# Two last attention groups, two chunks of batch 1's split input and 70 due times put elsewhere in a planned one-core kernel

## The chip, the core and the metric

The program runs on one core of a Trainium2 chip. The time is the device time of the whole program in microseconds (us), the median over several executions. The engines of the core are TensorE (PE in the profile, with its weight loads as PEld), VectorE (DVE), ScalarE (ACT), GpSimd (POOL) and SyncE (SP), which here only issues transfers. Each engine runs its own list of instructions in order and waits on semaphores for the others.

## The reference, cut to what is computed

```python
# 1 attention with feature maps: 8 batches, 8 heads, 576 rows, head_dim 64, 128 features
proj = q_or_k @ w_phi;  proj -= max(abs(proj), -1);  phi = concat(exp(proj), exp(-proj))
kv = einsum('bhsf,bhsd->bhfd', phi_k, v);  z = sum(phi_k, axis=2)
x = (phi_q @ kv) / (phi_q @ z + 1e-6)            # heads joined: x is [8, 576, 512]
# 2 gated mixer
gate = sigmoid(sum over k < 5 of conv_w[k] * shifted(x, k))
x = (gate * (x @ w_val)) @ w_out
# 3 Fourier mixing and MLP
u  = x + real(fft(fft(x, axis=1), axis=2))
un = (u - mean(u)) / sqrt(var(u) + 1e-6)
return u + maximum(un @ w_ch1, 0) @ w_ch2
```

Everything is float32. Products that need the precision are made of a high and a low part of the inputs, three matmuls for each product.

## The kernel before

The kernel has two halves. The first, up to 286 us of the trace, is attention: batches and heads in groups, in an order written out by hand. Of its steps only the end matters here. `emit_yT` (line 306) transposes the features of q on TensorE (tile `yt`), `emit_qE` lets ScalarE take the exponentials (`qe`), `emit_KV` (line 284) accumulates `kv` and copies it to `kvT`, `emit_num` makes the numerator (`nm`), VectorE divides (`xs`), `emit_XT` transposes back (`xt`, line 349), `emit_xT` copies that out of its bank (`xT`), and SP stores it to the scratch `x_scr`, from where the mixer loads its input `xf`.

The second half is one list of 4629 operations. The functions `note_...` write them down in program order with what each reads and writes, and `place_ops` (line 1165) turns them into the lists of the engines: backwards it gives each operation a due time, then it goes forward and takes, on each engine, the operation that is ready with the earliest due time. An operation can be allowed on two engines (letters `v`, `p`, `a`, `m`, `d` for VectorE, GpSimd, ScalarE, TensorE, SP); the forward pass then chooses. `key_at` and `free` say how far resources and engines are already taken when the list begins.

For each batch b of eight the list holds:

- `note_x` (line 519): the input is split in four chunks c into a high part (ScalarE) and a low part (VectorE or GpSimd, `o_lo`), into the tile pair `xh`. One pair serves all batches, so a chunk is written only after the batch before has read it for the last time.
- `note_taps`, `note_V` (line 545): the gate, and for each of four column groups m the product `val` = x @ w_val, in two halves of the sequence, one in each of the banks `val0` and `val1`. VectorE multiplies by the gate into `gv` and back into the bank, copies a column, and adds and subtracts the halves into `gs`. When that is done the bank is free for the next product. The split of `gs` is `ge`.
- `note_W`: the product of `ge` with w_out, into the banks `ps`. `note_FD` is the transform over features (tiles `f`, `Y`, rests `md`, `xr`, `rem`), `note_SD` the one over the sequence.
- `ln_first`: the LayerNorm of the first rows, whose mean is a product of `sh` and `sl` (a row block's high and low part) with ones. `note_sums` works off sums of weights (`ws`, four additions on GpSimd, a store `s_scr<-ws` and a load `ws<-s_scr`), beside everything else.

The tail of attention (`note_tail`: the last groups' `yt`, `kv`, `nm`, `xt`) is part of this list; the generator `tail` is stepped once for each m of batch 0. Which tiles exist when is set by `STAGES` (line 657): an operation with a key of stage 2 runs only after `open_mix2` (line 449) has made that stage's tiles, and `open_mix2` begins with six memsets on GpSimd. The list then goes on to the MLP, which fills the second half of the span.

## Time and profile before

| | us |
|---|---|
| median of 3 runs | 1323.23 (1321.36 to 1324.6) |
| profiled execution, its own time | 1319.18 |
| span of that execution in the trace | 1317.1 |
| PE busy | 1285.5 |
| DVE busy | 1134.1 |
| ACT busy | 919.0 |
| POOL busy | 791.9 |

The profile is of one execution; what lies outside its span is 2.1 us. PE busy counts matmuls from their start to a modelled end. A gap on an engine is printed in brackets, with the releaser: the engine and the tile whose instruction ended the wait. The granted clock (PEclk) is 1.00 at 2.4 GHz and 0.50 at 1.2 GHz.

### The profile page before, as it was taken

What the parts mean: (1) busy time and instruction counts of PE and PEld (TensorE: products, weight loads), DVE (VectorE), ACT (ScalarE), POOL (GpSimd) and SP (SyncE); (2) the same over time, 40 slices, a digit from 0 to 9 for tenths busy, and PEclk for the clock granted to TensorE, in tenths of its full rate; (3) what the DMA queues carried; (4) which work ended last, traced back from release to release, by engine and by line L of the source; (5) the groups of instructions that cost most, each with busy time, mean ns of one, the idle gap of its engine ahead of it and who ended that gap; (6) DMA issues with size and microseconds to landing.
All of it is one profiled execution on the core that took longest, in us unless ns stands there. A gap on an engine that the chain in (4) does not pass through costs nothing.

```text
span 1317.1 us, 30740 instructions
## 1 busy us (share of the span) xinstructions
PE 1285.5 (98%) x11952; PEld 1183.3 (90%) x11952; DVE 1134.1 (86%) x1771; ACT 919.0 (70%) x1718; POOL 791.9 (60%) x661
## 2 busy tenths in 40 slices
PE   8999999998999998999999999999999999999998
PEld 7999899988999998998888888888888888889997
DVE  6888888878889889779989989998989888888785
ACT  6888999774556546466867687767677676777662
POOL 4868889333557666464665755597458856583321
PEclk9999999998999999999999999999999999999999
DMA  8689999522342442528433653356333743345322
GB/s 309 207 287 308 319 300 296 189 83 89 137 165 88 147 155 89 177 89 276 138 102 102 222 159 104 103 160 218 104 103 117 241 123 100 105 149 182 105 84 89
DMA packets 147005, 214.62 MB, mean 163 GB/s; under 512 B 18854, under 2 KB 105382, under 8 KB 146860
## 3 DMA queue, kind: packets, MB, share of 16 engines
q1 hardware_dynamic: 142400, 203.06, 47.5%
q10 hardware_dynamic: 4460, 9.62, 2.0%
q8 instruction: 93, 1.52, 0.5%
q14 instruction: 52, 0.43, 0.1%
HBM read 165.63 MB, written 46.99 MB: 161 GB/s over the span
## 4 chain that ended last, share of the span: by engine, by line
PE 86%; DVE 6%; ACT 4%; DMA 2%; issue 1%; POOL 0%; SPq 0%; DVEq 0%; POOLq 0%; ACTq 0%
PE x L64 15%; PE cx L64 15%; PE ps L64 12%; PE cy L64 11%; PE y L64 8%; PE val L64 5%; PE kv L64 5%; PE pj L64 5%; PE nm L64 4%; PE z L64 4%; DVE acc L64 2%; PE yt L311 2%; PE xt L349 1%; ACT qe L64 1%; DMA r<-s_scr 1%
## 5 line engine op out<-in xcount | busy, mean ns | idle before, releaser
L64 POOL TENSOR_TENSOR r<-r 128x256 fp32r<-128x256 f32 (+1 forms) x301 | 293.4, 992 | 245.6 <-ACT r L64 229.2
L64 ACT ACTIVATE r<-r 128x256 fp32r<-128x256 f32 (+1 forms) x420 | 195.3, 487 | 53.4 <-DMA r<-s_scr 49.7
L64 PE MATMUL x<-un,r 128*128 128x462 f32 (+1 forms) x960 | 221.2, 371 | 2.2 <-ACT c L64 1.4
L64 PE MATMUL cx<-h,r 128*128 128x462 f32 (+1 forms) x960 | 213.9, 371 | 1.1 <-DVE acc L64 1.1
L64 PEld LDWEIGHTS x<-un,r 128*128 128x128 f32 x960 | 180.4, 188 | 23.5 <-ACT c L64 1.8
L64 PEld LDWEIGHTS cx<-h,r 128*128 128x128 f32 x960 | 180.2, 188 | 22.1 <-DVE acc L64 1.8
L64 PE MATMUL cy<-h,r 128*128 128x462 f32 (+1 forms) x720 | 159.9, 370 | 0.0
L64 PEld LDWEIGHTS cy<-h,r 128*128 128x128 f32 x720 | 135.3, 188 | 15.1
L64 PE MATMUL val<-xh,wv 128*128 128x290 f32 x768 | 118.0, 303 | 10.6 <-DVE gs L64 4.7
L64 PEld LDWEIGHTS val<-xh,wv 128*128 128x128 f32 x768 | 108.5, 193 | 13.7 <-DVE gs L64 5.6
L64 PE MATMUL y<-un,r 128*128 128x462 f32 (+1 forms) x480 | 113.9, 372 | 0.4 <-DVE h L64 0.4
L64 PE MATMUL ps<-ge,wo 128*128 128x290 f32 x768 | 107.3, 297 | 2.0 <-DVE x L64 1.1
L64 PEld LDWEIGHTS ps<-ge,wo 128*128 128x128 f32 x768 | 104.5, 189 | 2.8 <-DVE x L64 1.3
L270 DVE TENSOR_REDUCE m<-pj 128x6 f32<-128x768 f32 x96 | 91.5, 953 | 15.4 <-PE pj L64 14.8
L64 PEld LDWEIGHTS y<-un,r 128*128 128x128 f32 x480 | 90.0, 188 | 11.4 <-DVE h L64 1.1
L64 DVE SCALAR_TENSOR_TENSOR acc<-xf,cw,acc 128x576 f32<-128x576 f32 x112 | 91.4, 816 | 10.0 <-ACT acc L64 9.1
L64 DVE TENSOR_TENSOR acc<-cx,acc 128x924 f32<-128x924 f32 (+1 forms) x80 | 88.9, 1112 | 11.6 <-PE cx L64 10.2
L271 DVE TENSOR_TENSOR y<-pj,m 128x768 f32<-128x768 f32 x96 | 91.9, 958 | 6.9 <-DVE m L270 0.5
L64 PE MATMUL kv<-vraw,ke 128*64 128x66 f32 x2560 | 88.1, 224 | 1.7 <-ACT kvT L64 1.7
L64 ACT ACTIVATE qe<-yt 128x768 f32<-128x768 f32 x96 | 72.6, 812 | 23.4 <-PE yt L311 23.4
L64 ACT ACTIVATE h<-z 128x462 fp32r<-128x462 f32 (+1 forms) x120 | 66.4, 553 | 29.8 <-DVE z L64 26.1
L64 PE MATMUL pj<-wp,kqraw 64*128 64x128 f32 x1152 | 80.8, 287 | 6.0 <-DMA kqraw<-in_k_dram 4.0
(174 smaller groups left out, 2752.5 us busy)
## 6 DMA issues: line engine op xcount, KB each, us to landing
r<-s_scr SPq DMA_DIRECT2D x280, 128.0 KB, 2.4
r<-s_scr SPq DMA_DIRECT2D x140, 256.0 KB, 2.6
raw<-in_w_ch_dram SPq DMA_DIRECT2D x32, 512.0 KB, 6.0
vraw<-in_v_dram SPq DMA_DIRECT2D x32, 330.0 KB, 6.1
u_scr<-u ACTq DMA_DIRECT2D x8, 1152.0 KB, 6.3
kqraw<-in_k_dram SPq DMA_DIRECT2D x46, 192.0 KB, 4.1
kqraw<-in_q_dram SPq DMA_DIRECT2D x46, 192.0 KB, 3.7
s_scr<-mt SPq DMA_DIRECT2D x32, 256.0 KB, 5.2
```

What stands on the lines that cost most here:

```text
L64: return lambda *a, **k: f(*(resolve(x) for x in a), **{n: resolve(x) for n, x in k.items()})
L270: nc.vector.tensor_reduce(out=m, in_=pv, axis=AX.X, op=ALU.max, apply_absolute_value=True)
L271: nc.vector.tensor_tensor(out=y, in0=pv, in1=m.unsqueeze(3).to_broadcast([128, 2, CH, F]), op=ALU.subtract)
L311: nc.tensor.transpose(t[:, h, j * F:(j + 1) * F], y[:, h, j, :], ident)
L349: nc.tensor.transpose(t[:, 0, j * F:(j + 1) * F], x[:, j].rearrange("p h d -> p (h d)"), ident)
```

## The change

Six things are changed. The copy of the last `kv` is an operation of its own. The tail is stepped twice at m = 0 and m = 1 and not at m = 2 and 3. Chunks 0 and 1 of batch 1's split input go to other places: three slices of 576 columns of the tile of `Y` (now one tile for both halves of the feature transform) and one in the tile of `sh0` and `sl0` (now one tile, `sums0`). They get the key `xq` of stage 2, and batch 1's first product counts as a reader of `Y`, `sh0` and `sl0`, so nothing writes these before it is done. The eviction `xT` may go to VectorE or ScalarE. The planner starts with ScalarE taken for 1.4 us, VectorE for 0.7 and the bank `tr` until 1.4, and makes three backward passes instead of two. And a table MOVES shifts the due times of 70 operations (numbers 7 to 1498 of 4629) by multiples of 0.5 us, the largest by 191 us.

```diff
@@ -281,7 +281,12 @@
 
     KV_PARTS = [[[(0, 0), (1, 1), (2, 2)]], [[(3, 0), (4, 1)], [(5, 1), (6, 2)]], [[(7, 0), (8, 1), (9, 2)]]]
 
-    def emit_KV(i, part):
+    def copy_KV(u, b):
+        if b == 0:
+            kvT[u] = sm_p.tile([128, 4, 2, 65], F32, tag="kvT", name="kvT")
+        act.activation(out=kvT[u][:, :, b, :], in_=kvps.pop((u, b))[:, :, 0:65], func=ACTF.Copy)
+
+    def emit_KV(i, part, copy=True):
         u, g = divmod(i, NG)
         tv = vraw[u % 2]
         e = kE[i]
@@ -296,10 +301,8 @@
                     for p in HALVES:
                         mm(t[p, w, :], e[:, a, h, j, p], tv[:, h, slot, :],
                            start=slot % 5 == 0 and w == 0, stop=slot % 5 == 4 and w == 3, skip_group_check=True)
-            if slot % 5 == 4:
-                if b == 0:
-                    kvT[u] = sm_p.tile([128, 4, 2, 65], F32, tag="kvT", name="kvT")
-                act.activation(out=kvT[u][:, :, b, :], in_=kvps.pop((u, b))[:, :, 0:65], func=ACTF.Copy)
+            if slot % 5 == 4 and copy:
+                copy_KV(u, b)
         if part == len(KV_PARTS[g]) - 1:
             kE.pop(i)
 
@@ -452,12 +455,17 @@
         late["fs"] = x2.tile([128, 2, NE], F32, name="fs")
         late["c256"] = x2.tile([128, 5, 128], F32R, name="c256")
         late["r256"] = x2.tile([97, 2, NE], F32, name="r256")
+        sums = x2.tile([128, 2, HB], F32R, name="sums0")
+        Y = x2.tile([128, 2, 2, 2, NL], F32R, name="Y")
+        flat = Y.rearrange("p i j a l -> p (i j a l)")
+        late["x1", 0, 0], late["x1", 0, 1], late["x1", 1, 0] = (flat[:, S * i:S * i + S] for i in range(3))
+        late["x1", 1, 1] = sums.rearrange("p i s -> p (i s)")[:, 0:S]
         for i in range(2):
             late["f", i] = x2.tile([128, 2, 2, NE], F32R, name=f"f{i}")
-            late["Y", i] = x2.tile([128, 2, 2, NL], F32R, name=f"Y{i}")
+            late["Y", i] = Y[:, i]
             late["xr", i] = x2.tile([128, NE], F32R, name=f"xr{i}")
             late["rem", i] = x2.tile([128, NL], F32R, name=f"rem{i}")
-            late[("sh0", "sl0")[i]] = x2.tile([128, HB], F32R, name=("sh0", "sl0")[i])
+            late[("sh0", "sl0")[i]] = sums[:, i]
         late["T0"] = x2.tile([128, 2, HB], F32, name="T0")
         late["u256"] = x2.tile([97, S], F32, name="u256")
         late["u"] = x2.tile([128, 4, S], F32, name="u")
@@ -516,16 +524,23 @@
                 gps.tensor_tensor(out=acc[:, a], in0=acc[:, a], in1=t, op=ALU.add)
             yield
 
+    OVER_X = ["sh0", "sl0"] + [("Y", j, a, k) for j in range(2) for a in range(2) for k in range(2)]
+
+    def parts_of_x(b, c):
+        if b == 1 and c < 2:
+            return [later(("x1", c, k)) for k in range(2)], [("xq", c, k) for k in range(2)]
+        return [later(("xh", k))[:, c] for k in range(2)], [("xh", c, k) for k in range(2)]
+
     def note_x(b):
         t = later(("xf", b % 2))
         if b > 1:
             o_dma([(t[:, :, 4:], x_scr[b].rearrange("c p s -> p c s"))], [("x_scr", b)], [("xf", b % 2)], 1152)
         if b:
             for c in range(4):
-                h, l = (later(("xh", i))[:, c] for i in range(2))
+                (h, l), (hk, lk) = parts_of_x(b, c)
                 x = t[:, c, 4:]
-                o_hi(h, x, S, [("xf", b % 2)], [("xh", c, 0)])
-                o_lo("vp", l, x, h, S, [("xf", b % 2), ("xh", c, 0)], [("xh", c, 1)])
+                o_hi(h, x, S, [("xf", b % 2)], [hk])
+                o_lo("vp", l, x, h, S, [("xf", b % 2), hk], [lk])
 
     def note_taps(b, m):
         t, s = later(("xf", b % 2)) if b else x0, later(("sg", m % 2))
@@ -544,7 +559,7 @@
 
     def note_V(b, m):
         g, i = b % 2, m % 2
-        h, l = later(("xh", 0)), later(("xh", 1))
+        xp, xk = zip(*(parts_of_x(b, c) for c in range(4)))
         gate = later(("sg", i)).rearrange("p a s -> p (a s)")
         gv, gs = later(("gv", i)), later(("gs", i))
         for n in range(2):
@@ -555,9 +570,9 @@
                 def prod(e, p=p, sl=sl, part=part):
                     ws = slice(m * 128, (m + 1) * 128)
                     for c in part:
-                        mm3(p[:, 0:NE], (wv[0][:, c, ws], wv[1][:, c, ws]), (h[:, c, sl], l[:, c, sl]), c == 0, c == 3)
+                        mm3(p[:, 0:NE], (wv[0][:, c, ws], wv[1][:, c, ws]), (xp[c][0][:, sl], xp[c][1][:, sl]), c == 0, c == 3)
                 end = [("done", "V", n)] * (b == NB - 1 and m == 3 and part == (3,))
-                op("m", 0, prod, [("xh", c, k) for c in part for k in range(2)] + [("pv", n)] * (part[0] > 0), [("pv", n)] + end, 3 * len(part) * 0.134)
+                op("m", 0, prod, [k for c in part for k in xk[c]] + OVER_X * (b == 1 and part == (0, 1)) + [("pv", n)] * (part[0] > 0), [("pv", n)] + end, 3 * len(part) * 0.134)
             o_tt("v", (gv, p[:, 0:NE])[n], p[:, 0:NE], gate[:, sl], ALU.mult, NE, [("pv", n), ("sg", i)], [(("gv", i), ("pv", n))[n]])
         p = later(("pv", 1))
         op("v", 1, lambda e: vec.tensor_copy(out=p[:, NE:NE + 1], in_=gv[:, 0:1]), [("gv", i), ("pv", 1)], [("pv", 1)])
@@ -656,7 +671,7 @@
     BANKS = {"x0", "x1", "y", "z", "cx", "cy", "ps", "pv", "pa", "nm"}
     STAGES = {k: (a, b) for a, b, n in (
         (0, 0, "early"), (0, 1, "att tr nm"), (0, 2, "xf xh sg"), (1, 2, "pv pa gv gs ws ge0"), (1, 3, "ge1"),
-        (2, 3, "x2 f Y fs u u256 xr rem c256 r256 ps T0 sh0 sl0"), (3, 4, "un r0 c11 c12 c22 x0 y z"),
+        (2, 3, "xq x2 f Y fs u u256 xr rem c256 r256 ps T0 sh0 sl0"), (3, 4, "un r0 c11 c12 c22 x0 y z"),
         (4, 4, "B sh sl x1 cx cy h acc r1"), (3, 3, "third"),
     ) for k in n.split()}
 
@@ -1101,7 +1116,8 @@
         for m in range(4):
             note_taps(0, m)
             note_V(0, m)
-            next(tail, None)
+            for i in range((2, 2, 0, 0)[m]):
+                next(tail, None)
         for b in range(NB - 1):
             note_x(b + 1)
             for i, c in enumerate((0, 2, 1, 3)):
@@ -1159,8 +1175,17 @@
                 c2 = c2_units(t, pair)
         drain(c2)
 
-    key_at = {}
-    free = dict.fromkeys("mvapdxw", 0.0)
+    MOVES = {
+        7: 146, 32: 382, 54: -221, 58: -126, 80: 4, 100: -22, 122: 212, 241: 4, 252: 253, 272: -16, 273: -14, 278: 76,
...
+        1338: -12, 1348: 7, 1416: -64, 1431: -71, 1498: -103,
+    }
+    key_at = {"tr": 1.4}
+    free = dict(dict.fromkeys("mvapdxw", 0.0), a=1.4, v=0.7)
 
     def place_ops():
         n = len(ops)
@@ -1198,7 +1223,7 @@
             now -= ops[i][0].get("m", 0)
             if "m" in ops[i][0] or ops[i][9]:
                 place[i] = now
-        for _ in range(2):
+        for _ in range(3):
             till = dict.fromkeys("mvapdw", total)
             rest = [len(s) for s in succ]
             heap = []
@@ -1224,6 +1249,8 @@
                     if not rest[p]:
                         open_up(p)
             ends = [min(due[i] for i in range(n) if part[i] > k) if k < 4 else 1e9 for k in range(5)]
+        for i, v in MOVES.items():
+            due[i] += 0.5 * v
         left = [len(p) for p in pred]
         ready = {e: set() for e in "mvapd"}
         at = [max([key_at.get(k, 0.0) + lat for k in ops[i][2] + ops[i][3]], default=0.0) for i in range(n)]
@@ -1315,7 +1342,8 @@
         nk = ["kvT"]
 
         def kv(i):
-            op("m", 0, lambda e: emit_KV(i, 0), ["early"], ["kv"], 24 * 0.058)
+            op("m", 0, lambda e: emit_KV(i, 0, False), ["early"], ["kv"], 24 * 0.058)
+            op("a", 260, lambda e: copy_KV(i // NG, 1), ["kv"], ["kvT"])
 
         def yt(i):
             op("m", 0, lambda e: emit_yT(i), ["early"], ["tr"], 2 * CH * 0.11)
@@ -1330,7 +1358,7 @@
 
         def xt(i):
             op("m", 0, lambda e: emit_XT(i, ps_tr, "tr"), [("xs", i % 3), "att"], ["tr"], CH * 0.11)
-            op("a", 128 * CH, lambda e: emit_xT(i, "a"), ["tr"], [("xT", i % 2)])
+            op("va", 128 * CH, lambda e: emit_xT(i, e), ["tr"], [("xT", i % 2)])
             t = Late(lambda: xT[i])
             o_dma([(o, t[:, k]) for b, o, k in x_parts(i)], [("xT", i % 2)], [("x_scr", b) for b, o, k in x_parts(i)], 192)
 
```

The instructions of the engines change as follows. TensorE has the same 8946 matmuls; VectorE goes from 1773 to 1769 instructions, ScalarE from 1736 to 1738 (table loads from 7 to 9), GpSimd from 666 to 670. From about 650 us on the lists are the same to the end on every engine. In the lists below x4 stands for four alike in a row. A number behind a tile's name tells tiles of one name apart: of the pairs, val_5436 and val_5459 are the bank val0 of the two kernels, val_5439 and val_5462 the bank val1, ps_5803 and ps_5741 the bank ps3.

The first place is TensorE at the end of attention, around 286 us. Before:

```order
L64 MATMUL nm<-kvT,qe 64x65 x24
L64 MATMUL kv<-vraw,ke 64x66 x16
L349 MATMUL xt<-ident,xs 128x128 x3
L311 MATMUL yt<-ident,y 128x128 x12
L64 MATMUL kv<-vraw,ke 64x66 x24
L64 MATMUL val_5436<-xh,wv_118 128x290 x2
```

and now:

```order
L64 MATMUL nm<-kvT,qe 64x65 x24
L64 MATMUL kv<-vraw,ke 64x66 x16
L352 MATMUL xt<-ident,xs 128x128 x3
L314 MATMUL yt<-ident,y 128x128 x6
L64 MATMUL kv<-vraw,ke 64x66 x24
L64 MATMUL nm<-kvT,qe 64x65 x24
L314 MATMUL yt<-ident,y 128x128 x6
L64 MATMUL val_5459<-xh,wv_118 128x290 x2
```

The two last transposes `yt` were one piece; a `kv` and an `nm` group now lie between them.

The second place is GpSimd from the end of batch 0's split to the start of batch 1's. Before:

```order
L64 TENSOR_TENSOR xh<-x_114,xh 128x576 x2
L64 TENSOR_TENSOR ws<-ws 128x256 x5
L64 TENSOR_TENSOR xh<-xf,xh 128x576 x3
L64 TENSOR_TENSOR ge<-gs,ge 128x580
L64 TENSOR_TENSOR ws<-ws 128x256 x5
L467 MEMSET c_5785 128x640
L467 MEMSET r_5786 97x580
```

and now, where `Y<-xf,Y` is the low part of batch 1's chunk 0:

```order
L64 TENSOR_TENSOR xh<-x_114,xh 128x576 x2
L64 TENSOR_TENSOR ws<-ws 128x256 x8
L475 MEMSET c_5725 128x640
L475 MEMSET r_5726 97x580
L475 MEMSET xr_5730 128x290
L475 MEMSET xr_5733 128x290
L475 MEMSET rem_5731 128x258
L475 MEMSET rem_5734 128x258
L64 TENSOR_TENSOR Y<-xf,Y 128x576
L64 TENSOR_TENSOR xh<-xf,xh 128x576 x2
L64 TENSOR_TENSOR ge<-gs,ge 128x580
```

The memsets of `open_mix2` have come ahead of batch 1's low parts, and with them eight sums in a row. SP at the same place, the stores of `xT` and the sums' transfers, before:

```order
L706 DMA x_scr_72<-xT 128x384
L706 DMA s_scr_0_75<-ws 128x1024
L706 DMA ws<-s_scr_0_83 128x4x256
L706 DMA x_scr_71<-xT 128x384
L706 DMA x_scr_71<-xT 128x192
L706 DMA x_scr_72<-xT 128x192
L706 DMA x_scr_72<-xT 128x384
L706 DMA s_scr_0_83<-ws 128x4x256
L706 DMA ws<-s_scr_1_76 128x1024
```

and now:

```order
L721 DMA ws<-s_scr_0_75 128x1024
L721 DMA xf<-x_scr_67 128x4x576
L721 DMA s_scr_0_75<-ws 128x1024
L721 DMA ws<-s_scr_0_83 128x4x256
L721 DMA x_scr_72<-xT 128x384
L721 DMA x_scr_71<-xT 128x384
L721 DMA x_scr_71<-xT 128x192
L721 DMA x_scr_72<-xT 128x192
L721 DMA s_scr_0_83<-ws 128x4x256
L721 DMA x_scr_72<-xT 128x384
L721 DMA ws<-s_scr_1_76 128x1024
```

The last store of `xT` (x_scr_72, 128x384) now stands behind the store s_scr_0_83 of the second group of sums.

The third place is the second mean of a LayerNorm block, around 495 us. TensorE before:

```order
L64 MATMUL ps_5803<-sh_5791,ones 128x462
L64 MATMUL ps_5803<-sl_5796,ones 128x462
L64 MATMUL val_5436<-xh,wv_118 128x290 x2
L64 MATMUL val_5436<-xh,wv_119 128x290
L64 MATMUL val_5439<-xh,wv_118 128x290 x2
L64 MATMUL val_5439<-xh,wv_119 128x290
L64 MATMUL val_5436<-xh,wv_118 128x290 x2
L64 MATMUL val_5436<-xh,wv_119 128x290
L64 MATMUL val_5439<-xh,wv_118 128x290 x2
L64 MATMUL val_5439<-xh,wv_119 128x290
L64 MATMUL ps_5803<-ge,wo 128x290 x12
```

and now:

```order
L64 MATMUL ps_5741<-sums_5727,ones 128x462 x2
L64 MATMUL ps_5738<-ge,wo 128x290 x12
L64 MATMUL ps_5740<-ge,wo 128x290 x12
L64 MATMUL ps_5741<-ge,wo 128x290 x12
L64 MATMUL val_5462<-xh,wv_118 128x290 x2
```

The mean's product was followed by 12 matmuls of `val`, now by 24 of `ge`. VectorE there, before:

```order
L64 COPY val_5439<-gv 128x1
L64 TENSOR_TENSOR x_114<-x_114,T_5797 128x462
L64 TENSOR_TENSOR sl_5796<-x_114,sh_5791 128x462
L64 TENSOR_TENSOR fs<-x_5783,ps_5802 128x290
L64 TENSOR_TENSOR fs<-x_5783,ps_5803 128x290
L64 TENSOR_TENSOR ge<-gs,ge 128x580
L64 SCALAR_TENSOR_TENSOR acc<-xf,cw,acc 128x2x288
L64 TENSOR_TENSOR gs<-gv,val_5439 128x290 x2
```

and now:

```order
L64 TENSOR_TENSOR x_114<-x_114,T_5735 128x462
L64 TENSOR_TENSOR val_5462<-val_5462,acc 128x290
L64 TENSOR_TENSOR gv<-val_5459,acc 128x290
L64 COPY val_5462<-gv 128x1
L64 TENSOR_TENSOR gs<-gv,val_5462 128x290 x2
L64 TENSOR_TENSOR fs<-x_5723,ps_5740 128x290
L64 TENSOR_TENSOR fs<-x_5723,ps_5741 128x290
```

The `gs` that frees the bank val1 stood seven rows behind the copy into it, and now stands right behind it.

## Rows read from the trace of the kernel before

**Rows 1.** Page, part 1: busy us, share of the span and count of each engine.

```profile
PE 1285.5 (98%) x11952; PEld 1183.3 (90%) x11952; DVE 1134.1 (86%) x1771; ACT 919.0 (70%) x1718; POOL 791.9 (60%) x661
```

**Rows 2.** Stretches (us): span, then busy us of PE, PEld, DVE, ACT, POOL.

```profile
286.00:322.00 36.00, 29.94 (x341) 28.05 (x340) 27.55 (x57) 18.59 (x29) 11.87 (x12) 0.91 0.34 120
322.00:400.00 78.00, 75.10 (x564) 74.12 (x564) 67.56 (x131) 41.67 (x89) 43.04 (x45) 1.00 0.39 137
400.00:470.00 70.00, 69.38 (x519) 68.15 (x519) 63.24 (x120) 41.08 (x82) 47.29 (x41) 1.00 0.35 122
470.00:512.00 42.00, 36.05 (x264) 34.76 (x264) 37.01 (x68) 24.54 (x47) 26.28 (x23) 1.00 0.42 137
...
598.00:650.00 52.00, 49.84 (x236) 43.98 (x236) 48.31 (x80) 42.46 (x93) 27.65 (x31) 1.00 0.68 224
```

**Rows 3.** TensorE's timeline: start, us, line, out<-in, count [idle before, releaser].

```profile
287.80 0.87 PE L311 MATMUL yt<-ident,y 128*128 128x128 f32 x6 [1.60 <-ACT qe L64]
...
296.75 2.67 PE L64 MATMUL val<-xh,wv 128*128 128x290 f32 x18 [0.36 <-DVE gs L64]
...
311.68 0.55 PE L349 MATMUL xt<-ident,xs 128*128 128x128 f32 x3 [1.34 <-ACT xT L64]
311.98 0.38 PE L64 MATMUL val<-xh,wv 128*128 128x290 f32 x1
314.99 5.92 PE L64 MATMUL val<-xh,wv 128*128 128x290 f32 x23 [2.63 <-DVE xh L64]
```

**Rows 4.** ScalarE's timeline, end of attention.

```profile
292.74 1.28 ACT L64 ACT_TABLE_LOAD   x1
```

**Rows 5.** GpSimd's timeline, 290 to 331 us.

```profile
294.20 3.18 POOL L64 TENSOR_TENSOR ws<-ws 128x256 f32<-128x256 f32 x4 [13.48 <-DMA ws<-s_scr]
309.44 0.74 POOL L64 TENSOR_TENSOR ws<-ws 128x256 f32<-128x256 f32 x1 [12.06 <-DMA ws<-s_scr]
310.18 4.14 POOL L64 TENSOR_TENSOR xh<-xf,xh 128x576 fp32r<-128x576 f32 x3
...
328.55 0.62 POOL L467 MEMSET xr<- 128x290 f32 x2
329.11 0.57 POOL L467 MEMSET rem<- 128x258 f32 x2
```

**Rows 6.** SP's issues on the timeline, and landing of tile xT's stores, 280 to 330.

```profile
287.55 0.43 SPq L706 DMA_DIRECT2D ws<-s_scr  x1
...
301.04 0.32 SPq L706 DMA_DIRECT2D s_scr<-ws  x1
305.62 0.37 SPq L706 DMA_DIRECT2D ws<-s_scr  x1
...
DMA to landing us min/median/max: 1.7/1.7/1.8
```

**Rows 7.** Two stretches of 2 and 4 us; the third number from the end is PEclk.

```profile
316.00:318.00 2.00, 2.00 (x10) 2.00 (x9) 1.89 (x4) 0.00 (x0) 1.84 (x4) 0.50 0.00 0
...
504.00:508.00 4.00, 0.86 (x6) 0.86 (x7) 4.00 (x9) 2.80 (x6) 3.92 (x4) 1.00 0.00 0
```

**Rows 8.** TensorE's timeline, later waits, 345 to 610 us.

```profile
345.64 2.96 PE L64 MATMUL val<-xh,wv 128*128 128x290 f32 x20 [1.54 <-DVE xh L64]
...
498.40 1.86 PE L64 MATMUL ps<-ge,wo 128*128 128x290 f32 x12 [1.07 <-DVE x L64]
...
507.14 1.07 PE L64 MATMUL val<-xh,wv 128*128 128x290 f32 x6 [3.21 <-DVE gs L64]
...
606.88 1.53 PE L64 MATMUL x<-un,r 128*128 128x462 f32 x6 [0.73 <-DVE c L64]
...
609.84 1.53 PE L64 MATMUL x<-un,r 128*128 128x462 f32 x6 [1.43 <-ACT c L64]
```

**Rows 9.** VectorE's timeline, 501 to 507 us: val's copy and gs.

```profile
501.67 0.16 DVE L64 COPY val<-gv 128x1 f32<-128x1 f32 x1
...
506.28 0.81 DVE L64 TENSOR_TENSOR gs<-gv,val 128x290 f32<-128x290 f32 x2
```

5 rows, old and new, of the table MOVES are left out of this document.

## The prediction

> **What bounds the kernel now.** I began with the share of each engine in the span. TensorE's matmuls are busy 98% of it [rows 1], so only the missing 2% can be won, unless the change removes matmuls; it removes none (both kernels issue the same 8946 instructions of that kind, in the same shapes). So the question is where TensorE stood still, and whether it stands still elsewhere afterwards. The second view is the table of stretches [rows 2], which I cut where the work changes: 286 us is where the attention order ends and the planned list begins, 650 us is where the lists of the two kernels become identical again to the last instruction. Idle in a row is the stretch minus PE's busy time: 6.06 us in 286 to 322, 2.90 in 322 to 400, 0.62 in 400 to 470, 5.95 in 470 to 512, 2.16 in 598 to 650; together 17.7 us (512 to 598 has none). What lies before 286 and after 650 isn't touched.
>
> The third view is TensorE's timeline in the first of these stretches [rows 3]. It idles 1.60 us for the activation that frees the transpose bank, 0.36 for a gs of VectorE, 1.34 for an eviction xT, and 2.63 before batch 1's product, for the low part of its input. That is 5.93 of the 6.06. The last row has a second loss: 23 matmuls took 5.92 us, 0.257 each, where 18 of the same shape had taken 2.67, 0.148 each. So 2.5 us went to the clock. In all 20.2 us (17.7 and 2.5) are the most that this change can give.
>
> **The change part by part.** All sums are against the profiled execution (1319.18 us, its span 1317.1 and 2.1 around it); the median before is 1323.23, 4.05 higher, and what is won is taken off either.
>
> *The end of attention.* Before, the two last transposes yt stood next to each other, and the second waited 1.60 us for the qe that reads the first. Now a kv and one nm group stand between them; both are ready, nothing is added, and the 1.60 goes. On ScalarE the two sigmoids now come before the last two qe, with a table load on either side. Of the change's two more table loads one stands here, the other near 440 us; a load took 1.28 us [rows 4]. The last qe is then ready near 294.2 and its nm is reached near 299, so this is hidden; without that cover it would cost 1.28. The copy of the last kvT is only split off, at no cost for the same reason. The xT wait (1.34) goes, because the three transposes xt behind it now have V products between them. One new hand-over is in sight, at the last V product of batch 0: gate times value for the bank before is done only just then, 0 to 0.85 us. So TensorE gets to batch 1's product between 308.7 (311.98, where its first matmul started, less 3.30 of waits) and 309.5.
>
> *Batch 1's input in other tiles.* Chunks 0 and 1 of x no longer wait for batch 0's last reads of xh, so ScalarE and VectorE can split them early. But the tiles belong to the next stage, whose opening puts six memsets on GpSimd ahead of chunk 0's low part, and those of xr lie over the buffers of xT: they wait until the last store of xT has landed. On SP that store now stands behind the second store of the weight sums, which waits for GpSimd's second group of four additions. This chain is worked out from two groups [rows 5, 6]. The first load of ws is issued by 287.55. It lands after 3.82 us (305.62 to 309.44, the later load) or 6.65 (287.55 to 294.20, where the big load of xf stood ahead of it; now it stands behind). Then four additions 3.18, store 4.58 (301.04 to 305.62, where the next load is let go), load 3.82, four additions 3.18, two issues on SP 0.7, the xT store's landing 1.7 (the row for xT) up to the 4.58 of the other store, four memsets behind it 0.62 + 0.57, and the low part 1.38 (4.14 for three). The sum is 311.1 with the short values and 316.8 with the long. I take 312.0: both short values were measured on the nearer transfers, and 0.9 is left for what they don't cover. Batch 1's product then waits 2.5 to 3.3 us, about as long as before, but it begins 3 us earlier (312.0 against 314.99). At 0.148 us its 24 matmuls end at 315.6; before, they ended at 320.9. **Gain 5.3.** With the long chain and the low clock (24 x 0.257) they end at 323.0, a loss of 2.1.
>
> *The clock.* The granted clock was 0.50 from 316 to 318 us although PE was busy for all of it, after a stretch with many short waits; but near 504 to 508, where PE was busy for 0.86 of 4 us, it stayed at 1.00 [rows 7]. So one wait of 3 us doesn't have to bring the 1.2 GHz level. I take 2.4 GHz in the sum, since three of the four waits before batch 1 are gone; 1.2 GHz in the 24 matmuls costs 2.6.
> The Trainium skill ("TensorE: Matmul & The Clock Gate", section "What's actually happening") says that the throttled state is the default and that activity releases it. By that rule a wait that remains is paid twice, first as idle time and then as slow matmuls, and the sum would be the 9.1 us of the first rival; the trace agrees with it after 314.99 and shows no slow matmuls after 507.14.
>
> *Batches 1 to 4, 322 to 470 us.* Here the new order and the split between GpSimd and VectorE have 3.52 idle us to take from [rows 2], the largest a wait of 1.54 for the low part of batch 2's input [rows 8]. Its first two chunks can now be written early, since batch 1 doesn't read these places, and the last two have some 4.8 us of other matmuls ahead of them. Short gaps of three or four matmuls between two products on the same bank, of which there were three, are gone. I leave 1.0: **gain 2.5**, bounds 0 and 3.5.
>
> *470 to 512 us.* Two waits make up most of the 5.95: 1.07 for the LayerNorm's x and 3.21 for gs [rows 8]. The first: the mean's two matmuls were followed by 12 matmuls of V (1.8 us) and then by the bank's next use; now by 24 of W (3.6 us), which is 1.8 more cover than the old sum and more than the 1.07. The second: between the copy into val and the gs that frees it VectorE did six other instructions, and gs began 4.61 us after the copy did [rows 9]. In the new order gs stands right behind the copy. The next product on that bank is 30 matmuls (4.4 us) away, where it was 36. I leave 0.3: **gain 4.0**, bounds 0 and 4.3.
>
> *598 to 650 us.* The two waits of 0.73 and 1.43 before the MLP's first products [rows 8] go, because such products now stand inside the last W and sequence transforms. A new wait of up to 1.2 is possible at the first of them, whose low part VectorE writes late; half of it is left: **gain 1.5**, bounds 0.9 and 2.2.
>
> The 70 shifted due times act through the order alone and are in these terms. What the rows of before can't show is small waits between units in another order: the two middle stretches of before left 0.62 and 2.90 us [rows 2]; I take off 1.6 for it.
> Sum: 5.3 + 2.5 + 4.0 + 1.5 - 1.6 = **11.7 us**, so 1307.5 for the profiled execution and 1311.5 for the median.
>
> **The rivals.** (1) *The clock isn't regained*: 11.7 - 2.6 = 9.1, 1314.1. For it: 314.99. Against: 504 to 508. (2) *The wait at batch 1 is only moved*: the chain over memsets, SP and the sums comes at its long end. The first term turns from 5.3 to -2.1; 4.3 are left, 1318.9. For it: 6.65 and 4.58 are measured too. Against: both had other bytes ahead of them. (3) *VectorE is the bound behind TensorE*: it was busy 37.01 of 42 us and 48.31 of 52 in the stretches of the last two terms [rows 2], so a reordered list only moves those waits. 11.7 less 5.5 leaves 6.2, 1317.0. Against: in 512 to 598 it kept up. (4) *Slower*: the product units of batches 1 to 7 (28 of them) share two banks, each freed by VectorE. If the new order brings its gv and gs late at all of them, the kernel is slower by 4 us from (13.3 + 4) / 28 = 0.62 us each; at the 0.73 of the smallest long wait shown [rows 8] it would cost 20.4, and 1323.2 - 13.3 + 20.4 = 1330.3. Against: no stretch of before comes near. (5) *The change does nothing*: the tiles or due times leave the waits where they are, each gain met by a new wait, 1323.
>
> **How the numbers follow.** A chance of 0.40 for the forecast, 0.20 for (1), 0.12 for (2), 0.14 for (3), 0.06 for (4), 0.08 for (5). A difference under 0.3%, 4 us here, can't be told from none. Faster by more than that: the forecast, (1), three quarters of (2) and nearly all of (3): 0.81. Within: the rest of (2) and (3), and (5) but for a hundredth: 0.12. Slower: (4) and that hundredth: 0.07. The range goes from 1304, nearly all of the 20.2 won, to 1320, which takes in (1) to (3).
>
> **What would show it.** Right: in the new profile yt, xt and the first gs have no wait; the x part of batch 1 starts near 312 with a granted clock of 1.00 behind it; PE idles under 1 us between 470 and 512; the stretch from the end of the mixer on is as long as before. Wrong: memsets on GpSimd ending after 314, slow matmuls at batch 1, a wait for gv or gs that repeats from unit to unit, or VectorE at 95% in 400 to 520.

## The result and the profile after

| | before | changed |
|---|---|---|
| median, four runs of each | 1322.3 us (1320.0 to 1324.6) | 1303.6 us (1303.0 to 1304.3) |
| ratio | | 0.9861, 95% interval 0.984 to 0.9883 |
| span of the profiled execution | 1317.1 | 1302.5 |

The kernel is 18.7 us faster by the medians. Forecast were 11.7, at 1311.5, and a range from 1304; the time lies 0.4 us below it.

The span differs by 14.6 only, because attention, the same in both, took longer in the changed kernel's profiled execution. One wait shows most of it. Before:

```profile
71.75 1.15 PE L64 MATMUL kv<-vraw,ke 128*64 128x66 f32 x32 [0.32 <-ACT kvT L64]
```

and in the changed kernel:

```profile
73.25 1.15 PE L64 MATMUL kv<-vraw,ke 128*64 128x66 f32 x32 [1.92 <-ACT kvT L64]
```

So I compare the planned list alone, from the first of the last two transposes `yt` to a product `x` of the MLP behind which both orders are equal. These are the rows before (start, duration, count):

```profile
285.38 0.82 PE L311 MATMUL yt<-ident,y 128*128 128x128 f32 x6
...
649.38 1.40 PE L64 MATMUL x<-un,r 128*128 128x462 f32 x6
```

and now:

```profile
287.71 0.82 PE L314 MATMUL yt<-ident,y 128*128 128x128 f32 x6
...
634.44 1.40 PE L64 MATMUL x<-un,r 128*128 128x462 f32 x6
```

The list took 364.00 us and takes 346.73: **17.3 us shorter**, where the forecast had 11.7. The stretches of the changed kernel, in the columns of [rows 2] and at its times, but for the last, which ends where the lists become equal:

```profile
286.00:322.00 36.00, 32.38 (x413) 31.12 (x410) 27.71 (x60) 22.87 (x35) 16.86 (x22) 0.95 0.41 135
322.00:400.00 78.00, 77.11 (x579) 76.30 (x578) 71.40 (x137) 42.59 (x92) 51.93 (x46) 1.00 0.46 154
400.00:470.00 70.00, 69.53 (x521) 68.86 (x522) 64.97 (x123) 42.07 (x85) 42.73 (x39) 1.00 0.42 143
470.00:512.00 42.00, 42.00 (x318) 41.78 (x317) 40.77 (x76) 26.71 (x51) 34.90 (x31) 1.00 0.27 101
...
598.00:636.00 38.00, 37.69 (x180) 33.41 (x180) 36.73 (x59) 32.57 (x74) 24.92 (x28) 1.00 0.71 226
```

PE idles 3.62, 0.89, 0.47, 0.00 and 0.31 us in them, 5.3 together; before it was 17.7. Its waits now, and what follows the longest, on the timeline of TensorE as in [rows 3]:

```profile
291.41 0.87 PE L314 MATMUL yt<-ident,y 128*128 128x128 f32 x6
...
308.87 1.88 PE L64 MATMUL val<-xh,wv 128*128 128x290 f32 x12 [0.54 <-DVE gs L64]
...
313.96 1.09 PE L64 MATMUL val<-Y,wv 128*128 128x290 f32 x3 [3.08 <-POOL Y L64]
```

The waits for qe, for xT and for the first gs are gone. One wait of over 1 us is left, 3.08 us at batch 1's product, and GpSimd's timeline shows what it is:

```profile
294.38 3.17 POOL L64 TENSOR_TENSOR ws<-ws 128x256 f32<-128x256 f32 x4 [11.33 <-DMA ws<-s_scr]
304.31 3.50 POOL L64 TENSOR_TENSOR ws<-ws 128x256 f32<-128x256 f32 x4 [6.76 <-DMA ws<-s_scr]
...
311.39 0.62 POOL L475 MEMSET xr<- 128x290 f32 x2 [2.49 <-ACT xh L64]
311.95 0.57 POOL L475 MEMSET rem<- 128x258 f32 x2
312.48 1.42 POOL L64 TENSOR_TENSOR Y<-xf,Y 128x576 fp32r<-128x576 f32 x1
```

and SP's issue of the last store of xT, with the landing times of tile xT's stores between 280 and 330 us:

```profile
308.31 0.46 SPq L721 DMA_DIRECT2D x_scr<-xT  x1
...
DMA to landing us min/median/max: 1.6/1.8/3.0
```

The second group of sums ends at 307.81, the last store of xT is issued half a microsecond later, and the memsets of xr start 3.08 us later and end at 312.5; only then comes `Y<-xf,Y`, the low part that TensorE waits for. The bracket at 311.39 names ScalarE, which is the releaser the view infers. Among the semaphores that the first memset of xr waits for is the store's own, since xr lies over the buffer that the store reads; the store landed at 311.25, 2.9 us after its issue, and GpSimd went on at 311.28. Behind the wait the granted clock (third number from the end) fell, to 0.50 and 0.71:

```profile
314.00:316.00 2.00, 2.00 (x8) 2.00 (x9) 0.93 (x2) 0.10 (x1) 2.00 (x2) 0.50 0.00 0
316.00:318.00 2.00, 2.00 (x13) 2.00 (x12) 0.04 (x1) 0.00 (x0) 2.00 (x2) 0.71 0.00 0
```

### The profile page after: what moved, and what is told of

It reads as the page before. It is cut to its first block, busy times and chain, and to the rows that moved or that the text cites. A ratio compares the mean times of both kernels' runs of the same rounds, so it can differ in the third digit from the quotient of the medians.

```text
span 1302.5 us, 30766 instructions
## 1 busy us (share of the span) xinstructions
PE 1280.2 (98%) x11952; PEld 1181.3 (91%) x11952; DVE 1126.5 (86%) x1767; ACT 918.2 (70%) x1720; POOL 795.6 (61%) x665
## 3 DMA queue, kind: packets, MB, share of 16 engines
q8 instruction: 93, 1.52, 0.5%
## 4 chain that ended last, share of the span: by engine, by line
PE 87%; DVE 4%; DMA 3%; ACT 3%; POOL 1%; issue 1%; SPq 0%; DVEq 0%; POOLq 0%; ACTq 0%
PE x L64 14%; PE cx L64 14%; PE ps L64 12%; PE cy L64 11%; PE y L64 7%; PE val L64 6%; PE kv L64 5%; PE pj L64 5%; PE nm L64 5%; PE z L64 4%; PE yt L314 2%; PE xt L352 2%; DMA r<-s_scr 1%; DVE acc L64 1%; DMA s_scr<-ws 1%
## 5 line engine op out<-in xcount | busy, mean ns | idle before, releaser
L64 POOL TENSOR_TENSOR r<-r 128x256 fp32r<-128x256 f32 (+1 forms) x306 | 299.3, 995 | 249.8 <-ACT r L64 224.7
L64 PE MATMUL val<-xh,wv 128*128 128x290 f32 x720 | 107.5, 299 | 1.6 <-DVE gs L64 1.5
L64 PEld LDWEIGHTS val<-xh,wv 128*128 128x128 f32 x720 | 99.9, 189 | 2.7 <-DVE gs L64 2.3
L64 PEld LDWEIGHTS kv<-vraw,ke 128*64 128x64 f32 x2560 | 81.0, 139 | 6.9 <-ACT kvT L64 3.8
```

What stands on the lines that cost most here:

```text
L64: return lambda *a, **k: f(*(resolve(x) for x in a), **{n: resolve(x) for n, x in k.items()})
```

## The experiments

A list length below is measured as above, from the first `yt` to that `x`. The kernel before has 364.00, the changed one 346.73 and, in a second profile of the same kernel, 346.55. A list length is that of one execution, and not all repeat so well: the kernel with the late memsets had 343.51 and 345.21, and the part from `yt` to the W products at 475.43, which is in the same order in the kernel before and in the two made from it, took 190.1, 188.5 and 189.7 us.

| kernel | list, us | median, us |
|---|---|---|
| without the 70 shifts | 368.14 | 1324.3 |
| with the old tiles for batch 1 | 364.13 | 1320.7 |
| shifts below 700 alone | 360.69 | 1315.9 |
| shifts above 700 alone | 358.93 | 1314.5 |
| memsets behind batch 1's low parts | 343.51, again 345.21 | 1300.7, again 1301.1 |
| memsets twice | 349.09 | 1305.8, one execution |
| transform six matmuls sooner | 348.60 | 1304.8, one execution |
| before, gs sooner | 365.60 | 1322.9 |
| before, gs and fs sooner, cover | 369.08 | 1327.3, one execution |

### Without the shifted due times

```diff
-        for i, v in MOVES.items():
-            due[i] += 0.5 * v
```

> The changed kernel without the 70 shifted due times; tail, tiles and planner settings stay. Theory A (the due times carry the stretch 470 to 512 and the short gaps between products on one bank, the tail and the tiles carry the start of the mixer): 1308 to 1313 us; a wait for gs or gv of over 2 us near the second mean of a LayerNorm block, where 12 instructions stand again between the copy into the bank and its gs, and several waits of 0.2 to 0.6 where only 3 matmuls lie between two products. Theory B (the due times only trim): 1304 to 1306.

1324.3 us, ratio to before 1.0016 (0.9998 to 1.0035): nothing of the gain is left. The start has the tail and the tiles, and neither yt nor xt waits. Two of the waits on TensorE, and the clock behind the second:

```profile
315.52 1.48 PE L64 MATMUL val<-xh,wv 128*128 128x290 f32 x5 [2.25 <-POOL xh L64]
...
505.06 1.82 PE L64 MATMUL val<-xh,wv 128*128 128x290 f32 x6 [6.84 <-DVE gs L64]
```

```profile
504.00:506.00 2.00, 0.94 (x4) 0.94 (x5) 1.97 (x5) 0.69 (x1) 1.92 (x3) 0.50 0.00 0
```

The 6.84 us stand at the second LayerNorm mean, where I had seen 12 instructions between the copy and gs. Theory A is right in kind and far too mild: the list is 21.4 us longer than with the shifts, 4.1 longer than before.

### With the old tiles

```diff
-        if b == 1 and c < 2:
+        if b == 99:
-... + OVER_X * (b == 1 and part == (0, 1)) + ...
+... + ...
```

> The changed kernel with batch 1's chunks 0 and 1 in the old tile xh, all else as changed. Theory A (the tiles end the wait for batch 0's last reads, worth 4 to 5 us at batch 1): 1308 to 1312, with a wait for xh of about 3 us or more at batch 1. Theory B (what came before batch 1, the tail alone, gave that gain): within 1.5 us of 1303.6.

1320.7 us, ratio 0.9993 (0.9977 to 1.0009), far above theory A's 1308 to 1312. The wait for xh at batch 1 is back, as theory A has it, and two more that it doesn't name:

```profile
313.56 2.78 PE L64 MATMUL val<-xh,wv 128*128 128x290 f32 x10 [5.14 <-DVE xh L64]
...
393.19 1.82 PE L64 MATMUL val<-xh,wv 128*128 128x290 f32 x6 [3.63 <-DVE gs L64]
...
506.13 1.82 PE L64 MATMUL val<-xh,wv 128*128 128x290 f32 x6 [3.47 <-DVE gs L64]
```

The six matmuls behind 393.19 and 506.13 took 1.82 us each, the 1.2 GHz level (the granted clock was 0.50 from 393 to 395 and from 506 to 510 us; at 0.134 they take 0.96 with the modelled end of the last). The planner then has other ready times and, with the same shifts, makes another order; that one waits for gs at two later places. So tiles and shifts don't add up: with the new tail and planner settings in all three kernels, either alone is worth nothing against before, both together 17.3. What the tail and the settings give without either was not run.

### Part of the shifts

```diff
-            due[i] += 0.5 * v
+            if i < 700:      # the other kernel: if i > 700
+                due[i] += 0.5 * v
```

> The changed kernel with the 26 shifted due times of operations below 700 alone, so with the order of the first three batches as changed and what comes later planned without shifts. Theory A (the gain of each stretch comes from the shifts of its own operations): no wait over 1 us from batch 1's start to 400 us, a wait of 2 us or more near the second mean of the LayerNorm block, 1310 to 1316 us. Theory B (a good start is enough): 1304 to 1307.

> The changed kernel with the 44 shifted due times of operations above 700 alone. Theory A: the start as without shifts (waits of 2.3 us at batch 1 and 1.8 near 384 us), the stretch of the LayerNorm with a wait under 1, 1308 to 1314 us. Theory B (the late shifts fit only the order that the early ones lead to): a wait of 3 us or more near the LayerNorm's second mean, 1317 to 1324.

Ratios to before 0.9946 (0.9926 to 0.9966) and 0.9942 (0.9917 to 0.9967). With the early shifts alone the list goes as in the changed kernel up to 400 us and then waits near the LayerNorm, twice for 1.24 us where theory A expected 2 or more once:

```profile
497.33 1.90 PE L64 MATMUL val<-xh,wv 128*128 128x290 f32 x12 [1.24 <-DVE gv L64]
500.46 1.73 PE L64 MATMUL val<-xh,wv 128*128 128x290 f32 x11 [1.24 <-DVE gs L64]
```

Further on it waits 1.05 us at 562 and 0.73 and 1.99 before the MLP's first products. With the late shifts alone the list keeps the wait of the start's order and has one of 3.00 near the LayerNorm, as theory B expected, at a time just above theory A's 1314:

```profile
383.67 2.70 PE L64 MATMUL val<-xh,wv 128*128 128x290 f32 x18 [1.76 <-DVE gv L64]
...
502.46 2.26 PE L64 MATMUL val<-xh,wv 128*128 128x290 f32 x9 [3.00 <-DVE gs L64]
```

Against the list without shifts the two are worth 7.5 and 9.2 us, and all together 21.4. Theory A (each stretch has its own shifts) holds for the first half, and for the MLP's first products, where the late shifts alone leave no wait. The stretch of the LayerNorm needs both, as theory B says.

### The memsets behind batch 1's low parts

```diff
-        for k in ("c256", "r256", ("xr", 0), ("xr", 1), ("rem", 0), ("rem", 1)):
-            nc.gpsimd.memset(f32(late[k]), 0.0)
+    def clear_rests():
+        for k in ("c256", "r256", ("xr", 0), ("xr", 1), ("rem", 0), ("rem", 1)):
+            nc.gpsimd.memset(f32(late[k]), 0.0)
...
                 o_lo("vp", l, x, h, S, [("xf", b % 2), hk], [lk])
+                if b == 1 and c == 3:
+                    low = ops[-1][1]
+                    ops[-1] = ops[-1][:1] + (lambda e, low=low: (low(e), clear_rests()),) + ops[-1][2:]
```

> The changed kernel with the six memsets of the next stage emitted behind the low parts of batch 1 instead of ahead of them; only GpSimd's order differs. Theory A (the memsets, held by the last store of xT, are what batch 1 waits 3.1 us for, and that wait is what lowers the clock): the wait falls under 0.5, the granted clock stays at 1.00 from 312 to 320, 1299 to 1300. Rival (the low part is late anyway, by its high part on ScalarE or the other low parts): a wait of over 1.5 stays and the time is 1302 or more.

GpSimd's timeline:

```profile
302.20 3.19 POOL L64 TENSOR_TENSOR ws<-ws 128x256 f32<-128x256 f32 x4 [7.51 <-DMA ws<-s_scr]
305.35 1.41 POOL L64 TENSOR_TENSOR Y<-xf,Y 128x576 fp32r<-128x576 f32 x1
...
312.21 0.63 POOL L477 MEMSET xr<- 128x290 f32 x2
```

TensorE's longest wait at batch 1, and its clock there:

```profile
309.95 0.53 PE L64 MATMUL val<-xh,wv 128*128 128x290 f32 x2 [0.89 <-DVE xh L64]
```

```profile
310.00:312.00 2.00, 1.80 (x11) 1.56 (x12) 1.97 (x4) 0.69 (x1) 2.00 (x3) 1.00 0.59 219
...
314.00:316.00 2.00, 1.96 (x15) 1.72 (x13) 1.76 (x6) 1.45 (x3) 2.00 (x2) 1.00 0.00 0
```

The low part now starts right behind the sums, at 305.35, and the wait for it is gone; 0.89 for another chunk's low part is what comes next. The clock stays at 1.00. The list is 3.2 us shorter than the changed kernel's, so theory A holds for the cause; its wait under 0.5 and its 1299 to 1300 were a little low. Both kernels again, on one chip:

> The kernel of e3_late_memsets again, for an interval against the changed kernel on one chip. If the wait and the low clock at batch 1 are worth what the first run's list showed (3.2 us), its median is 2.5 to 4 us under the changed kernel's.

> The changed kernel itself, for comparison on the same chip: 1302 to 1306 us, and in the profile again a wait of 3.1 us for the low part of batch 1 with the clock at 0.50 right behind it.

1301.1 us (ratio to before 0.9841, 0.9822 to 0.986) against 1305.6 (0.9881, 0.9863 to 0.9898); the intervals don't overlap, and the medians are 4.4 us apart, more than the 2.5 to 4 expected. The profile of the changed kernel shows the wait of 3.08 us again and 0.50 behind it. From `yt` to the end of batch 1's first 24 matmuls the late memsets took 27.9 us in both profiles, the changed kernel 30.9 and 31.0, so 3.0 and 3.1 are won there. The whole list was only 1.3 us shorter this time; three waits of 0.2 to 0.5 came later in that execution. This version beats both kernels.

### The memsets twice

```diff
             nc.gpsimd.memset(f32(late[k]), 0.0)
+            nc.gpsimd.memset(f32(late[k]), 0.0)
```

> The changed kernel with each of the six memsets done twice, 2.4 us more on GpSimd ahead of batch 1's low part. Theory A (a wait costs its idle time, what the restart takes, and the low clock behind it): a wait of 5.4 to 5.6 us at batch 1 where 3.1 were, the granted clock 0.50 for the whole of the next 4 us, and the list 3.5 to 4.5 us longer than in the changed kernel. Rival (a longer wait is caught up by work that is early later on): the list 1 us longer or less.

```profile
313.62 0.68 PE L64 MATMUL val<-Y,wv 128*128 128x290 f32 x3 [4.60 <-POOL Y L64]
```

The wait is 4.60 us, not 5.5: the memsets of c256 and r256 fit into the time for which those of xr wait for the store anyway, so only part of the 2.4 us counts. The idle time grew by 1.52 and the list by 2.36 (2.54 against the second profile), where theory A expected 3.5 to 4.5. The clock was 0.55 and 0.60 from 314 to 318 us, not 0.50 throughout. From `yt` to the end of batch 1's first 24 matmuls this kernel took 32.5 us, and 30.9 to 31.0 in the four profiles that have the changed kernel's order there: 1.5 are lost at the wait and not caught up later, so the rival falls, as far as one profile can tell.

### The gs of the kernel before, moved alone

```diff
+        sooner = [i for i in range(n) if ops[i][3] == [("ge", 0, 0, 1)]][3:4]
+        sooner += [i for i in range(n) if ops[i][3] in ([("gs", 0, 0)], [("gs", 0, 1)])][26:28]
+        for i in sooner:
+            e = next(e for j, e in order if j == i)
+            order.remove((i, e))
+            at = max(k for k, (j, _) in enumerate(order) if j in pred[i])
+            order.insert(at + 1, (i, e))
```

> The kernel before with one part alone: the gs of the unit at 506 us, and the ge before it that has to read the old gs, moved up on VectorE to stand two places behind the copy. Theory A (gs behind the copy is what removes the 3.21 us): wait under 0.5, 1318.5 to 1319.5 beside a kernel before of 1322.3. Theory B (the wait hides the chain fs, f to the feature transform behind it, and the changed kernel wins because other matmuls stand there): the wait moves to the feature transform, under 1 us won, 1321.5 to 1322.5.

1322.9 us, ratio 1.0009 (0.9991 to 1.0028). VectorE and TensorE there:

```profile
500.50 0.15 DVE L64 COPY val<-gv 128x1 f32<-128x1 f32 x1
...
503.02 0.85 DVE L64 TENSOR_TENSOR ge<-gs,ge 128x580 fp32r<-128x580 f32 x1 [1.76 <-ACT ge L64]
503.90 0.82 DVE L64 TENSOR_TENSOR gs<-gv,val 128x290 f32<-128x290 f32 x2
```

```profile
504.77 1.06 PE L64 MATMUL val<-xh,wv 128*128 128x290 f32 x6 [2.01 <-DVE gs L64]
...
506.77 0.50 PE L64 MATMUL ps<-ft,f 128*128 128x258 f32 x2 [0.59 <-ACT f L64]
508.27 0.58 PE L64 MATMUL ps<-ft,f 128*128 128x258 f32 x1 [0.99 <-POOL f L64]
```

gs can't follow the copy: it overwrites the old gs, which `ge` still has to read, and `ge` waits 1.76 us for its high part on ScalarE. The wait is 2.01 instead of 3.21, and the 1.2 us come back as 0.59 and 0.99 at the feature transform, for f. The clock stood at 0.50 from 508 to 510 us. From the three W products (475.43 before, 474.40 here) to the end of the transform (512.68 and 513.71) it took 39.3 us where the kernel before took 37.3. The list is longer by 1.6 us, but that is not the edit's price: ahead of those products, where the order is the same, this execution was 1.6 us shorter, and behind the transform 1.1 longer, with the clock at 0.55 near 611. Theory B.

### gs, fs and more cover in the kernel before

```diff
+        sooner = [i for i in range(n) if ops[i][3] == [("ge", 0, 0, 1)]][3:4]
+        gsw = [i for i in range(n) if ops[i][3] in ([("gs", 0, 0)], [("gs", 0, 1)])][26:28]
+        fsw = [i for i in range(n) if ops[i][3] in ([("fs", 0)], [("fs", 1)])]
+        sooner = [i for i in fsw if i in (903, 906)] + sooner + gsw + [1092, 1093]
...
```

> The kernel before with e4's edit, and besides the two fs at 504 us moved up ahead of the ge and gs, and the six matmuls of V that stood behind the feature transform moved ahead of it. Theory A (the gs and the chain from the last W product over fs and f to the transform both need their place, and matmuls to lie beside them): gs waits 1 us or less, the transform waits 0.5 to 1.5 for f, and the stretch from 475 us to the end of the transform is 1.5 to 2.5 us shorter than before. Theory B (nothing is to be had there without another order of everything): under 0.7.

```profile
512.46 3.27 PE L64 MATMUL val<-xh,wv 128*128 128x290 f32 x12 [3.02 <-DVE gs L64]
515.52 1.49 PE L64 MATMUL ps<-ft,f 128*128 128x258 f32 x6
```

The transform doesn't wait any more, but gs, behind fs, comes as late as before (3.02), and the twelve matmuls behind it took 3.27 us at the low clock. The stretch from the W products to the end of the transform, six matmuls of V included that stood behind it, took 42.9 us and before 38.1; nothing is won, which is theory B again. This execution had a wait of 2.04 us with the low clock behind it at 493.82, ahead of the edited place, so neither this nor its 369.08 is to be read as the price of the edit.

### The transform six matmuls sooner

```diff
+        FDS = [i for i in range(n) if ("f", 0, 0) in ops[i][2] and "m" in ops[i][0]]
+        for i in FDS[6 * 4:6 * 4 + 1]:
+            e = next(e for j, e in order if j == i)
+            was = order.index((i, e))
+            order.remove((i, e))
+            at = max(k for k, (j, _) in enumerate(order) if j in pred[i])
+            order.insert(at + 1, (i, e))
```

> The changed kernel with one product moved on TensorE: the first of the feature transform at 494.7 us now stands six matmuls earlier, so 27 matmuls of V lie between the last W product and it instead of 33. Theory A (what those 33 hide is the chain fs, f's high part, f's low part, which ended 0.3 us before the transform began): a wait of 0.4 to 0.6 us for f at the transform. Theory B (the chain has slack): no wait.

These are the changed kernel's own rows there, of TensorE and of GpSimd:

```profile
470.55 4.97 PE L64 MATMUL ps<-ge,wo 128*128 128x290 f32 x36
...
490.24 4.58 PE L64 MATMUL val<-xh,wv 128*128 128x290 f32 x33
494.66 0.88 PE L64 MATMUL ps<-ft,f 128*128 128x258 f32 x6
```

```profile
492.90 1.43 POOL L64 TENSOR_TENSOR f<-fs,f 128x580 fp32r<-128x580 f32 x1
```

f's low part ended at 494.33, the transform began at 494.66, and 33 matmuls (4.42 us, 0.134 each) lay between the last W product and it. With 27, TensorE's rows, the sixth matmul of the transform by itself, and GpSimd's low part:

```profile
488.86 3.78 PE L64 MATMUL val<-xh,wv 128*128 128x290 f32 x27
492.48 1.26 PE L64 MATMUL ps<-ft,f 128*128 128x258 f32 x6
```

```profile
493.35 0.39 PE L64 MATMUL ps<-ft,f 128*128 128x258 f32 x1
```

```profile
491.87 1.43 POOL L64 TENSOR_TENSOR f<-fs,f 128x580 fp32r<-128x580 f32 x1
```

The bracket shows no wait, but the group of six that took 0.88 us takes 1.26: 0.38 of stall inside it, just under the 0.4 to 0.6 that theory A expects. It stands ahead of the sixth matmul alone, which begins right behind the end of the low part (493.30). So theory A has the chain right and its slack wrong: in the changed kernel the sixth matmul begins at 495.26, 0.9 us behind the low part and not 0.3. A stall came even so because here the low part, counted from the start of those V matmuls, ended 0.35 us later. The list is 1.87 us longer than in the changed kernel; 0.37 of that stands at 483 us, ahead of the moved product, and 0.93 at the mean behind it, so the edit's own share is not settled.

## Why the prediction was wrong, point by point

**What bounds it** was right in kind: the list's gain, 17.3 us, is that of TensorE's waits and its clock. The 20.2 us that were called the most to be had were too few, as the price of a wait below shows.

**The end of attention** was right: no wait at yt, xt and the first gs; on ScalarE the two sigmoids, three table loads of 1.28 us and the last qe all lay beside TensorE's work. (Both additional loads stand here, at 291.04, 293.61 and 297.94 where the kernel before had one at 292.74; I had one of them near 440 us.) The one new hand-over took 0.54, inside its 0 to 0.85.

**Batch 1's start** was right in the chain, and its end was 0.4 us off: the low part ended at 313.9, which is 311.6 when the 2.33 us by which this list began later are taken off; I had 312.0. TensorE waited 3.08 us (2.5 to 3.3). The clock was wrong: I took rival 1 for the less likely, and the clock fell to 0.50 and 0.71, some 1.3 us by the starts of its matmuls instead of none. From yt to the end of batch 1's first 24 matmuls the list won 4.5 us, where 5.3 were forecast. That these memsets were the cause, and the clock's fall their consequence, is shown by the run that moved them.

**322 to 470 us** was right in size: up to the three W products at 475.43 before and 470.55 now the list won 7.2, so 2.7 in this stretch, where 2.5 were forecast, with two new waits of 0.28 and 0.96.

**470 to 512 us is the step that failed.** The first W product, the last product ahead of the wait in [rows 8] and the feature transform before:

```profile
475.43 5.01 PE L64 MATMUL ps<-ge,wo 128*128 128x290 f32 x36
...
502.96 0.96 PE L64 MATMUL val<-xh,wv 128*128 128x290 f32 x6
...
508.05 0.87 PE L64 MATMUL ps<-ft,f 128*128 128x258 f32 x6
```

From the first to the last of these the list had 32.6 us; now, with nine matmuls less in between, it has 24.1, so 7.3 are won at equal work, where the forecast was 4.0 and at most 4.3. Two things are wrong in it. The sum took two waits, 1.07 and 3.21; three more of 0.71, 0.76 and 0.20 stood in the same stretch and went too. By the starts of the rows (see the price of a wait below) these five cost 6.8 us, and 7.3 with a late second matmul behind each: all that was won. And the mechanism, gs standing right behind the copy, is not what removes the 3.21: in the order of before it can't stand there, for the ge that it waits for, and as near as its inputs allow it won nothing. What the changed kernel has is 33 matmuls of V between the last W product and the transform instead of 12, with the banks ready in that time and f's low part 0.9 us ahead of the matmul that needs it. The prediction doesn't name this chain over fs and f at all. That it is what the 33 matmuls hide is read from the rows; the run with six matmuls less beside it shows that it can stall the transform, and how much each of the two orders gives stays open. The order on VectorE and the order on TensorE had to change together; I read them from the new order as if each had its price.

**598 to 650 us**: both waits went and one of 0.31 came; with 512 to 598 the rest of the list won 2.8, where 1.5 were forecast. By the starts of the rows the two waits cost 2.7 and the new one 0.6, and three stalls too short for a bracket, at 534.7, 544.1 and 594.9 us before, cost 0.7 and are now one of 0.1.

**The price of a wait** was too low throughout. I took the idle time in the bracket. In the rows above six matmuls start at 502.96; at 0.134 each the next product would have started at 503.77, and it started at 507.14: 3.37 are lost where the bracket reads 3.21, because a matmul's row ends behind the point where the next can start (a single row here reads 0.29 us, and in a run of them one starts every 0.134). Over the 17 waits of the list before, worked out this way, 20.4 are lost where the brackets give 17.6; over the five now, 6.0 and 5.2. So the waits are worth 14.4 us and not 12.4, and with 1.2 of clock (2.5 lost before, 1.3 now) they are 15.6 of the 17.3. The other 1.7 are small pieces: behind nearly every wait the second matmul too starts about 0.1 us late (0.24 us after the first, not 0.134), and some stalls are too short for a bracket. By the brackets the range ended at 1304, nearly all of 20.2 won; by the starts of the rows there was more to win than that.

**The 1.6 us taken off** for waits that no row showed was counted twice: I had already left 1.0, 0.3 and half of a wait in the terms before it. The new waits outside batch 1 were 0.28, 0.96 and 0.31 in all, and they are in what the stretches won. Term by term the list won 4.5 (5.3 forecast), 2.7 (2.5), 7.3 (4.0) and 2.8 (1.5) with nothing to take off (1.6): 17.3 against 11.7.

**The rivals.** (1) came half true and was outweighed. (2) didn't come: the chain ran near its short end. (3) didn't: VectorE was busy 40.8 of 42 us from 470 on, more than before (93% from 400 to 520, under the 95 named as a sign), and TensorE didn't idle at all, so a high share of VectorE is no bound where its order fits. (4) and (5) didn't come in the changed kernel, but (5) is what it does without its shifts, and there single waits of 1 to 7 us did it, not 28 small ones.

**The reference.** 11.7 were taken off the median of the first three runs, 1323.23; by the fourth it is 1322.3. The profiles differ by less (14.9 us, from 1319.18 to 1304.29) since attention was slower in one: some 0.2% that belongs to neither kernel.

## What to carry to other kernels

Read a wait by the starts of the rows around it and not by the idle time printed: each cost 0.2 to 0.3 us more here, and the low clock behind some of them 1.3 to 2.7. The wait at the LayerNorm didn't go when the work that frees it was moved alone, so sum all waits of such a stretch or none, and don't add the parts of a change that share one plan. And when tiles of a new stage come sooner, look at what their opening puts in front: six memsets that nothing needs before the feature transform held the first product of a batch for 3 us, and moving them behind it was the cheapest edit of all.

## What was not expected of the hardware

The clock didn't follow the length of a single wait. After 3.21 us at 507.14 it stayed at 1.00 [rows 7]; after 3.08 at 313.96 it fell to 0.50, after 3.00 and 3.47 in two other kernels nine and six matmuls took 2.26 and 1.82 us, and after 2.01, 0.59 and 0.99 close together it was 0.50.

Nor did the same waits in the same order always end alike. The kernel before and the two made from it have the same list up to the edits, and behind the same wait at batch 1 the same 23 matmuls took 5.92 us before [rows 3], 5.71 with gs, fs and cover moved, and with gs alone moved

```profile
315.60 4.88 PE L64 MATMUL val<-xh,wv 128*128 128x290 f32 x23 [2.64 <-DVE xh L64]
```

Behind the waits of 0.73 and 1.43 at the MLP's first products the clock stayed at 1.00 from 610 to 614 us in the kernel before; with gs alone moved the same two waits came there and it was 0.55 and 0.60. So a fall can be worth 1 us more or less from one execution to the next, in the list of the kernel before too.

The Trainium skill ("TensorE: Matmul & The Clock Gate", section "What's actually happening") says that the throttled state is the default and activity releases it; the falls agree with that, and the wait at 507.14, with no fall behind it, shows that from the wait alone the price can't be told.
